# Half-length blocks for a chunked complex scan, with rotation tables read by broadcast

## The chip, the cores and the metric

The kernel runs on one core of one Trainium2 chip. The metric is the device time of the program in microseconds (us). Six runs of the kernel before took 205.23 to 207.02 us, with a median of 205.78 us.

The names used here: TensorE (PE in the profile) does matmuls and transposes and writes to PSUM. VectorE (DVE), ScalarE (ACT) and GpSimd (POOL) work on SBUF[...]. SyncE (SP) issues most of the DMAs. Each engine works through its own queue in order, and semaphores tie the queues together.

## The reference

The input x has 2048 rows of 512. It is normalised row by row, and three things are added: x itself, a diagonal complex state-space model (SSM) and a gated feed-forward network.

```python
def _A_ref(x, Lambda_re, Lambda_im, B_re, B_im, C_re, C_im, log_dt, Dskip):
    Lam = Lambda_re + 1j * Lambda_im
    dt = jnp.exp(log_dt)
    Lam_bar = jnp.exp(dt * Lam)
    B_bar = ((Lam_bar - 1.0) / Lam)[:, None] * (B_re + 1j * B_im)
    Bu = jnp.einsum("bld,pd->blp", x + 0j, B_bar)
    for t in range(L):                       # 2048 steps
        h = Lam_bar[None, :] * h + Bu[:, t, :]
    y = 2.0 * jnp.einsum("blp,dp->bld", hseq, C_re + 1j * C_im).real + x * Dskip

def _B_ref(x, w_gate, w_up, w_down):         # 512 -> 1376 -> 512
    return (_gelu(x @ w_gate) * (x @ w_up)) @ w_down

xn = _layernorm(x)
return x + _A_ref(xn, ...) + _B_ref(xn, ...)
```

The recurrence runs over the 2048 steps, separately for each of the 512 states.

## The kernel before

The 2048 steps are worked off in four chunks of CT = 512. States lie on partitions, 128 at a time, so there are KT = 4 groups of states, and time lies along the free dimension. One chunk of a state array is therefore a tile of 128 partitions by 4 x 512 = 2048 elements.

**The scan.** The complex recurrence is turned into two real ones. Each input is rotated back by the angle of its step, then a real scan with the factor r, the magnitude of Lam_bar, runs over the real and the imaginary part, and the result is rotated forward. Ct and St hold the cosine and sine of step times angle. Qc, Qs and nQs hold the forward rotation with the factor of B_bar folded in. coef holds r, with a zero at the first step of each state group, so that one scan instruction can run through all four groups. What is carried from one chunk to the next is the last column of the scan's results gre and gim, turned by the angle of a whole chunk and multiplied by r. It is added into the first column of the next chunk's input (lines 438 to 445).

**Setup.** Line 125 makes the row of step numbers (iota_f). The parameters arrive as a small tile vec_kp, which TensorE transposes (line 224) and VectorE copies to vec (226). From vec come dt (243, Exp), thn (245, turns per step), r (249, Exp), then turns, rounding and fraction (253 to 259), and Abs, Sin and Cos on ScalarE (276 to 281). B is transposed on TensorE in eight groups of four blocks (219) and copied out of PSUM (221), by VectorE or ScalarE, whichever the planner chose. Line 203 does the same for the normalised x of the first chunk; its PSUM pool holds one buffer, that of B's two.

**A chunk.** emit_v makes V, the input of the scan, in eight PSUM groups (real and imaginary part for each state group), which ScalarE copies out (363). emit_gu makes eleven pairs of groups, gate (372) and up (376), of four matmuls each. ScalarE takes the gelu of the gate (G, 381) and copies the up part (U, 382); VectorE multiplies them into H (388). All these groups share five PSUM buffers (ps_mm); G and U have three buffers each. The layer norm of chunks 2 and 3 is also done by ScalarE between them (173, 181), with its rstd by POOL (186). emit_ssm is VectorE's work: rotation (424 to 429), carry (438 to 445), two scans (448, 452), forward rotation into Hs (458 to 463). emit_output (399 to 406) adds everything up on TensorE, in four output groups of 24 matmul instructions a chunk, one chunk later: output of chunk c comes after V and gate/up of chunk c + 1.

**What sets the order.** The program is written engine-free of order; a planner puts each engine's instructions in a fixed sequence at build time, by its own estimates and by priorities. Blocks under hp() have a high priority and move ahead of ordinary ones as soon as the planner takes their inputs for ready. The order of a queue is then fixed, and an engine whose next instruction waits does nothing else.

Of the kernel before, what the change touches and what calls it, by code (L numbers as in the profile page):

```python
# [21 lines left out]
def kernel(  # L22
# [25 lines left out]
    CT = 512  # L48
    NCH = L // CT
    TPC = CT // P  # L50
    NFT = (F + P - 1) // P
    FSZ = [min(P, F - i * P) for i in range(NFT)]
    EPS = 1e-5
# [156 lines left out]
    ln_stats_dve(0)  # L210
    xnT_of[0] = ln_finish(0, use_pe=True)

    bT_re = const.tile([P, DC, NS], BF16, name="bT_re")
    bT_im = const.tile([P, DC, NS], BF16, name="bT_im")
    for bT, bn in ((bT_re, b_nat[0]), (bT_im, b_nat[1])):
        for dc in range(DC):
            pb = ps_b.tile([P, KT, P], BF16, name="pb", tag="b")
            for k in range(KT):
                nc.tensor.transpose(pb[:, k, :], bn[:, k, dc * P:(dc + 1) * P], ident[:])  # L219
            with hp():  # L220
                nc.any.tensor_copy(out=bT[:, dc, :], in_=pb[:].rearrange("p k q -> p (k q)"))

    pvec = ps_b.tile([P, 4 * KT], BF16, name="pvec", tag="b")
    nc.tensor.transpose(pvec[:], vec_kp[:], ident[0:4 * KT, 0:4 * KT])
    vec = small.tile([P, 4, KT], F32, name="vec")
    nc.vector.tensor_copy(out=vec[:].rearrange("p j k -> p (j k)"), in_=pvec[:])
    ps_b_cm.__exit__(None, None, None)
    lam_re = vec[:, 0, :]
    lam_im = vec[:, 1, :]
    logdt = vec[:, 2, :]  # L230
# [9 lines left out]
    nc.vector.memset(halfpi[:], math.pi / 2.0)  # L240

    dt = sm("dt")
    nc.scalar.activation(out=dt[:], in_=logdt, func=ACTF.Exp)
    thn = sm("thn")
    nc.vector.scalar_tensor_tensor(out=thn[:], in0=dt[:], scalar=INV_2PI, in1=lam_im, op0=ALU.mult, op1=ALU.mult)  # L245
    a_re = sm("a_re")
    nc.vector.tensor_tensor(out=a_re[:], in0=dt[:], in1=lam_re, op=ALU.mult)
    r = sm("r")
    nc.scalar.activation(out=r[:], in_=a_re[:], func=ACTF.Exp)

    turns = setup.tile([P, KT, CT], F32, name="turns")
    for k in range(KT):
        nc.vector.tensor_scalar(out=turns[:, k, :], in0=iota_f[:], scalar1=thn[:, k:k + 1], scalar2=None,
                                op0=ALU.mult)
    kk = setup.tile([P, KT, CT], F32, name="kk")
    nc.vector.tensor_scalar(out=kk[:], in0=turns[:], scalar1=ROUND_MAGIC, scalar2=ROUND_MAGIC,
                            op0=ALU.add, op1=ALU.subtract)
    frac = kk
    nc.vector.tensor_tensor(out=frac[:], in0=turns[:], in1=kk[:], op=ALU.subtract)
    th2 = sm2("th2")  # L260
    nc.vector.tensor_copy(out=th2[:, 0:KT], in_=thn[:])
    nc.vector.tensor_scalar(out=th2[:, KT:2 * KT], in0=thn[:], scalar1=float(CT), scalar2=None, op0=ALU.mult)
    k2 = sm2("k2")
    nc.vector.tensor_scalar(out=k2[:], in0=th2[:], scalar1=ROUND_MAGIC, scalar2=ROUND_MAGIC,
                            op0=ALU.add, op1=ALU.subtract)
    fr2 = sm2("fr2")
    nc.vector.tensor_tensor(out=fr2[:], in0=th2[:], in1=k2[:], op=ALU.subtract)

    afrac = turns
    St = const.tile([P, KT, CT], BF16, name="St")  # L270
    Ct = const.tile([P, KT, CT], BF16, name="Ct")
    afr2 = sm2("afr2")
    sn2 = sm2("sn2")
    cs2 = sm2("cs2")
# [8 lines left out]
    s1 = sn2[:, 0:KT]  # L283
    cTt = cs2[:, KT:2 * KT]
    sTt = sn2[:, KT:2 * KT]

    for c in range(1, min(N_DVE_LN, NCH)):
        ln_stats_dve(c)
# [35 lines left out]
    nf2im = sm("nf2im")  # L324
    nc.vector.tensor_scalar(out=nf2im[:], in0=f2im[:], scalar1=-1.0, scalar2=None, op0=ALU.mult)

    Qc = const.tile([P, KT, CT], BF16, name="Qc")
    Qs = const.tile([P, KT, CT], BF16, name="Qs")
    nQs = const.tile([P, KT, CT], BF16, name="nQs")
    coef = const.tile([P, KT, CT], F32, name="coef")  # L330
    qt = setup.tile([P, KT, CT], F32, name="qt")
    qt2 = setup.tile([P, KT, CT], F32, name="qt2")

    def emit_tables():
        for k in range(KT):
            nc.vector.tensor_scalar(out=qt[:, k, :], in0=St[:, k, :], scalar1=nf2im[:, k:k + 1], scalar2=None,
                                    op0=ALU.mult)
            nc.vector.tensor_scalar(out=qt2[:, k, :], in0=Ct[:, k, :], scalar1=f2im[:, k:k + 1], scalar2=None,
                                    op0=ALU.mult)
        for k in range(KT):  # L340
            nc.vector.scalar_tensor_tensor(out=Qc[:, k, :], in0=Ct[:, k, :], scalar=f2re[:, k:k + 1],  # L341
                                           in1=qt[:, k, :], op0=ALU.mult, op1=ALU.add)
            nc.vector.scalar_tensor_tensor(out=Qs[:, k, :], in0=St[:, k, :], scalar=f2re[:, k:k + 1],  # L343
                                           in1=qt2[:, k, :], op0=ALU.mult, op1=ALU.add)
        nc.vector.tensor_scalar(out=nQs[:], in0=Qs[:], scalar1=-1.0, scalar2=None, op0=ALU.mult)
        for k in range(KT):
            nc.vector.tensor_scalar(out=coef[:, k, :], in0=iota_f[:], scalar1=0.0, scalar2=r[:, k:k + 1],
                                    op0=ALU.mult, op1=ALU.add)
        nc.vector.memset(coef[:, :, 0:1], 0.0)

# [61 lines left out]

    g_prev = [None]

    def emit_ssm(c, V):
        vre = V[:, :, 0, :]
        vim = V[:, :, 1, :]
        m1 = rot.tile([P, KT, CT], BF16, name="m1")
        m2 = rot.tile([P, KT, CT], BF16, name="m2")
        m3 = rot.tile([P, KT, CT], BF16, name="m3")  # L420
        m4 = rot.tile([P, KT, CT], BF16, name="m4")
        ure = m1
        uim = m3
        nc.vector.tensor_tensor(out=m1[:], in0=Ct[:], in1=vre, op=ALU.mult)  # L424
        nc.vector.tensor_tensor(out=m2[:], in0=St[:], in1=vim, op=ALU.mult)
        nc.vector.tensor_tensor(out=ure[:], in0=m1[:], in1=m2[:], op=ALU.add)
        nc.vector.tensor_tensor(out=m3[:], in0=Ct[:], in1=vim, op=ALU.mult)
        nc.vector.tensor_tensor(out=m4[:], in0=St[:], in1=vre, op=ALU.mult)
        nc.vector.tensor_tensor(out=uim[:], in0=m3[:], in1=m4[:], op=ALU.subtract)
        if g_prev[0] is not None:  # L430
            gre_p, gim_p = g_prev[0]
            glr = gre_p[:, :, CT - 1]
            gli = gim_p[:, :, CT - 1]
            ca = stat.tile([P, KT], F32, name="ca")
            cb = stat.tile([P, KT], F32, name="cb")
            rire = stat.tile([P, KT], F32, name="rire")
            riim = stat.tile([P, KT], F32, name="riim")
            nc.vector.tensor_tensor(out=ca[:], in0=rcT[:], in1=glr, op=ALU.mult)
            nc.vector.tensor_tensor(out=cb[:], in0=rsT[:], in1=gli, op=ALU.mult)
            nc.vector.tensor_tensor(out=rire[:], in0=ca[:], in1=cb[:], op=ALU.subtract)  # L440
            nc.vector.tensor_tensor(out=ca[:], in0=rsT[:], in1=glr, op=ALU.mult)
            nc.vector.tensor_tensor(out=cb[:], in0=rcT[:], in1=gli, op=ALU.mult)
            nc.vector.tensor_tensor(out=riim[:], in0=ca[:], in1=cb[:], op=ALU.add)
            nc.vector.tensor_tensor(out=ure[:, :, 0], in0=ure[:, :, 0], in1=rire[:], op=ALU.add)
            nc.vector.tensor_tensor(out=uim[:, :, 0], in0=uim[:, :, 0], in1=riim[:], op=ALU.add)
        gre = gpool.tile([P, KT, CT], BF16, name="gre")
        gim = gpool.tile([P, KT, CT], BF16, name="gim")
        nc.vector.tensor_tensor_scan(out=gre[:].rearrange("p k t -> p (k t)"),  # L448
                                     data0=coef[:].rearrange("p k t -> p (k t)"),
                                     data1=ure[:].rearrange("p k t -> p (k t)"),  # L450
                                     initial=0.0, op0=ALU.mult, op1=ALU.add)
        nc.vector.tensor_tensor_scan(out=gim[:].rearrange("p k t -> p (k t)"),  # L452
                                     data0=coef[:].rearrange("p k t -> p (k t)"),
                                     data1=uim[:].rearrange("p k t -> p (k t)"),
                                     initial=0.0, op0=ALU.mult, op1=ALU.add)
        g_prev[0] = (gre, gim)
        Hs = hspool.tile([P, KT, 2, CT], BF16, name="Hs")
        nc.vector.tensor_tensor(out=m1[:], in0=Qc[:], in1=gre[:], op=ALU.mult)
        nc.vector.tensor_tensor(out=m2[:], in0=Qs[:], in1=gim[:], op=ALU.mult)
        nc.vector.tensor_tensor(out=Hs[:, :, 0, :], in0=m1[:], in1=m2[:], op=ALU.subtract)  # L460
        nc.vector.tensor_tensor(out=m3[:], in0=nQs[:], in1=gre[:], op=ALU.mult)
        nc.vector.tensor_tensor(out=m4[:], in0=Qc[:], in1=gim[:], op=ALU.mult)
        nc.vector.tensor_tensor(out=Hs[:, :, 1, :], in0=m3[:], in1=m4[:], op=ALU.subtract)
        return Hs

    pending = None
# [54 lines left out]
```

## Time and profile before

| | us |
|---|---|
| median of six runs | 205.78 |
| the profiled execution | 205.88 |
| its span, first to last instruction | 204.1 |
| TensorE busy | 184.5 (90%) |
| VectorE busy | 141.3 (69%) |
| ScalarE busy | 99.8 (49%) |
| POOL busy | 4.5 (2%) |
| first V matmul | 14.43 |
| V of the second chunk begins | 47.09 |
| first output group begins | 75.67 |
| mean granted TensorE clock | 0.983 |

The profile is one execution. Its strip of 40 slices shows the busy share of each engine in tenths, with the granted clock of TensorE in a row of its own. A row of groups names line, engine, operation, output<-inputs, shapes and count; behind the first bar stand total busy us and the mean ns of one, behind the second the idle time of the engine just before, with what ended it. The mean of one instruction is a little longer than the step from its start to the next one's: a VectorE product of 2048 elements has 1.22 us, and the next one starts 1.14 us after it. The table of waits adds up that idle time by who waited for whom. The chain of waits goes back from the last instruction to whatever released it, step by step.

### The profile page before, as it was taken

To read this page: it belongs to the slowest core of one execution; us is meant where nothing else is said; L and a number is where in the kernel's file an instruction comes from. 1 tells how busy PE (TensorE), PEld (TensorE's weight loads), DVE (VectorE), ACT (ScalarE), POOL (GpSimd) and SP (SyncE) were. 2 spreads that over 40 slices of the span, in tenths; PEclk is the share of its full clock that TensorE was granted. 3 is DMA by queue.
4 is the path that set the end of the run, shared out by engine and by line. 5 is a ranking of instruction groups with operands and counts; after the bars stand their busy time and mean duration, and the time that the engine had idled before them with its cause. 6 is when DMAs were issued, how large, how long until landed. Compare 5 with 4: busy or idle time off the path is not lost.

```text
span 204.1 us, 2468 instructions
## 1 busy us (share of the span) xinstructions
PE 184.5 (90%) x897; PEld 88.4 (43%) x915; DVE 141.3 (69%) x235; ACT 99.8 (49%) x187; POOL 4.5 (2%) x8
## 2 busy tenths in 40 slices
PE   1489749999997899999999999999999999999992
PEld 0364313444443344444444454444444444444441
DVE  6699899989999999991198999600699995000000
ACT  2176999897652644114998424116665541111111
POOL 0100100020000000000002000000000000000000
PEclk9999957999999999999999999999999999999999
DMA  5999972000002200103000040000000000001000
GB/s 168 315 386 358 212 165 51 2 0 0 3 0 43 60 0 0 50 31 112 16 0 5 8 97 26 26 29 26 0 0 0 3 0 26 26 26 54 26 26 27
DMA packets 19772, 12.25 MB, mean 60 GB/s; under 512 B 11216, under 2 KB 19760, under 8 KB 19760
## 3 DMA queue, kind: packets, MB, share of 16 engines
q1 hardware_dynamic: 19728, 12.10, 21.7%
q8 instruction: 7, 0.11, 0.2%
q14 instruction: 5, 0.04, 0.1%
q10 hardware_dynamic: 32, 0.00, 0.0%
HBM read 7.38 MB, written 2.10 MB: 46 GB/s over the span
## 4 chain that ended last, share of the span: by engine, by line
PE 64%; DVE 27%; DMA 2%; issue 2%; ACT 1%; POOL 1%; SPq 1%; ACTq 0%; DVEq 0%; POOLq 0%
PE po L399 19%; PE pu L376 10%; PE pg L372 10%; PE po L403 7%; PE pv L360 7%; PE po L402 6%; DVE H L388 2%; DMA bre_nat<-in_A_B_re_dram 2%; DVE gim L452 2%; DVE gre L448 2%; PE po L406 2%; PE po L404 2%; DVE Qs L343 1%; DVE Qc L341 1%; DVE xn L194 1%
## 5 line engine op out<-in xcount | busy, mean ns | idle before, releaser
L376 PE MATMUL pu<-xnT,wu 128*128 128x512 bf16 (+1 forms) x174 | 46.5, 389 | 6.7 <-ACT V L363 4.2
L372 PE MATMUL pg<-xnT,wg 128*128 128x512 bf16 (+1 forms) x172 | 45.3, 383 | 0.2
L399 PE MATMUL po<-wd,H 128*128 128x512 bf16 (+1 forms) x174 | 40.5, 379 | 0.1
L381 ACT ACTIVATE G<-pg 128x512 bf16<-128x512 f32 (+1 forms) x44 | 26.6, 605 | 27.1 <-DVE H L388 19.3
L410 ACT CAST osb<-po 128x512 bf16<-128x512 f32 x16 | 9.4, 587 | 52.7 <-PE po L406 52.7
L376 PEld LDWEIGHTS <-wu 128*128 128x128 bf16 (+1 forms) x176 | 17.9, 102 | 28.4 <-issue 9.2
L382 ACT CAST U<-pu 128x512 bf16<-128x512 f32 (+1 forms) x44 | 25.9, 590 | 4.3 <-PE pu L376 4.0
L372 PEld LDWEIGHTS <-wg 128*128 128x128 bf16 (+1 forms) x176 | 17.8, 101 | 21.4 <-issue 1.6
L403 PE MATMUL po<-cT_im,Hs 128*128 128x512 bf16 x64 | 24.2, 378 | 0.3
L399 PEld LDWEIGHTS <-H 128*128 128x128 bf16 (+1 forms) x176 | 16.7, 98 | 17.6
L363 ACT CAST V<-pv 128x512 bf16<-128x512 f32 x32 | 18.5, 584 | 7.3 <-PE pv L360 7.3
L402 PE MATMUL po<-cT_re,Hs 128*128 128x512 bf16 x58 | 22.0, 379 | 0.0
L388 DVE TENSOR_TENSOR H<-G,U 128x512 bf16<-128x512 bf16 (+1 forms) x44 | 18.0, 413 | 0.0
L360 PE MATMUL pv<-xnT,bT_re 128*128 128x512 bf16 x62 | 16.3, 379 | 0.8 <-DVE thn L245 0.7
L360 PE MATMUL pv<-xnT,bT_im 128*128 128x512 bf16 x62 | 16.2, 379 | 0.1
L424 DVE TENSOR_TENSOR m_1722<-Ct,V 128x2048 bf16<-128x2048 bf16 x1 | 1.2, 1226 | 13.9 <-ACT V L363 13.9
L403 PEld LDWEIGHTS <-Hs 128*128 128x128 bf16 x64 | 6.2, 97 | 7.6
L360 PEld LDWEIGHTS <-bT_im 128*128 128x128 bf16 x64 | 6.3, 98 | 7.5
L402 PEld LDWEIGHTS <-Hs 128*128 128x128 bf16 x64 | 6.2, 98 | 7.6
L360 PEld LDWEIGHTS <-bT_re 128*128 128x128 bf16 x64 | 6.2, 98 | 7.6 <-issue 0.7
L424 DVE TENSOR_TENSOR m_1362<-Ct,V 128x2048 bf16<-128x2048 bf16 x1 | 1.2, 1224 | 8.8 <-ACT V L363 8.8
L219 PE MATMUL pb<-ident,bre_nat 128*128 128x128 bf16 x16 | 2.2, 307 | 4.8 <-DMA bre_nat<-in_A_B_re_dram 4.3
(158 smaller groups left out, 198.9 us busy)
## 6 DMA issues: line engine op xcount, KB each, us to landing
out_dram<-osb SPq DMA_DIRECT2D x16, 128.0 KB, 1.7
x_c<-in_A_x_dram SPq DMA_DIRECT2D x3, 512.0 KB, 6.0
wd<-in_B_w_down_dram SPq DMA_DIRECT2D x1, 1280.0 KB, 12.9
wg<-in_B_w_gate_dram SPq DMA_DIRECT2D x1, 736.0 KB, 10.9
wu<-in_B_w_up_dram SPq DMA_DIRECT2D x1, 736.0 KB
wg<-in_B_w_gate_dram SPq DMA_DIRECT2D x1, 640.0 KB, 8.4
wu<-in_B_w_up_dram SPq DMA_DIRECT2D x1, 640.0 KB
x_c<-in_A_x_dram SPq DMA_DIRECT2D x4, 128.0 KB, 2.4
```

Of the source, the lines that this page charges most:

```text
L360: nc.tensor.matmul(pv[:], lhsT=bT[:, dc, k * P:(k + 1) * P], rhs=xnT[:, dc, :], start=(dc == 0), stop=(dc == DC - 1))
L363: nc.scalar.copy(out=V[:, k, part, :], in_=pv[:])
L372: nc.tensor.matmul(pg[0:fs, :], lhsT=wg[:, dc, ft * P:ft * P + fs], rhs=xnT[:, dc, :], start=(dc == 0), stop=(dc == DC - 1))
L376: nc.tensor.matmul(pu[0:fs, :], lhsT=wu[:, dc, ft * P:ft * P + fs], rhs=xnT[:, dc, :], start=(dc == 0), stop=(dc == DC - 1))
L381: nc.scalar.activation(out=G[0:fs, :], in_=pg[0:fs, :], func=ACTF.Gelu_apprx_tanh)
L382: nc.scalar.copy(out=U[0:fs, :], in_=pu[0:fs, :])
L388: nc.vector.tensor_tensor(out=H[0:fs, ft, :], in0=G[0:fs, :], in1=U[0:fs, :], op=ALU.mult)
L399: nc.tensor.matmul(po[:], lhsT=H[0:fs, ft, tsl], rhs=wd[0:fs, ft, :], start=first, stop=False)
L402: nc.tensor.matmul(po[:], lhsT=Hs[:, k, 0, tsl], rhs=cT_re[:, k, :], start=False, stop=False)
L403: nc.tensor.matmul(po[:], lhsT=Hs[:, k, 1, tsl], rhs=cT_im[:, k, :], start=False, stop=False)
L404: nc.tensor.matmul(po[:], lhsT=ident[:], rhs=x_tiles[c][:, i, :], start=False, stop=False)
L410: nc.scalar.copy(out=osb[:], in_=po[:])
```

## The change

The chunk stays at 512 steps, but the scan inside it goes by blocks of TB = 256 steps, NH = 2 to a chunk.

- All tables (Ct, St, Qc, Qs, nQs, coef and what they are made of) have 256 steps instead of 512. The whole-block angle is that of 256 steps.
- The eight table multiplies per chunk read a table twice, through a view (bc) with a step of zero over the two halves. V and Hs keep their layout and are read and written through a matching view (hk). The tiles m1 to m4, gre and gim are laid out half by half.
- Each scan is done in two instructions of 1024 elements, with a carry before each but the very first.
- In the text of the setup, the eight groups of B's transposes stand behind the parameter work and the tables; the parameter copy, dt, thn and the angle work stand under hp().

The first lines below set the new sizes; the parameter and angle part follows, then the tables, then the scan. Left out are the lines where only CT turned into TB in a shape and the unchanged formulas.

```diff
+    TB = 256
+    NH = CT // TB
...
-    bT_re = const.tile([P, DC, NS], BF16, name="bT_re")
-    bT_im = const.tile([P, DC, NS], BF16, name="bT_im")
-    for bT, bn in ((bT_re, b_nat[0]), (bT_im, b_nat[1])):
...
     pvec = ps_b.tile([P, 4 * KT], BF16, name="pvec", tag="b")
     nc.tensor.transpose(pvec[:], vec_kp[:], ident[0:4 * KT, 0:4 * KT])
     vec = small.tile([P, 4, KT], F32, name="vec")
-    nc.vector.tensor_copy(out=vec[:].rearrange("p j k -> p (j k)"), in_=pvec[:])
-    ps_b_cm.__exit__(None, None, None)
+    with hp():
+        nc.vector.tensor_copy(out=vec[:].rearrange("p j k -> p (j k)"), in_=pvec[:])
...
-    nc.scalar.activation(out=dt[:], in_=logdt, func=ACTF.Exp)
+    with hp():
+        nc.scalar.activation(out=dt[:], in_=logdt, func=ACTF.Exp)
+        nc.vector.scalar_tensor_tensor(out=thn[:], in0=dt[:], scalar=INV_2PI, in1=lam_im, op0=ALU.mult,
+                                       op1=ALU.mult)
...
-    turns = setup.tile([P, KT, CT], F32, name="turns")
-    for k in range(KT):
-        nc.vector.tensor_scalar(out=turns[:, k, :], in0=iota_f[:], scalar1=thn[:, k:k + 1], ...
+    with hp():
+        turns = setup.tile([P, KT, TB], F32, name="turns")
+        for k in range(KT):
+            nc.vector.tensor_scalar(out=turns[:, k, :], in0=iota_f[:, 0:TB], scalar1=thn[:, k:k + 1], ...
+        kk = setup.tile([P, KT, TB], F32, name="kk")
...
+        nc.vector.tensor_scalar(out=th2[:, KT:2 * KT], in0=thn[:], scalar1=float(TB), scalar2=None, op0=ALU.mult)
...
+    bT_re = const.tile([P, DC, NS], BF16, name="bT_re")
+    bT_im = const.tile([P, DC, NS], BF16, name="bT_im")
+    for bT, bn in ((bT_re, b_nat[0]), (bT_im, b_nat[1])):
+        for dc in range(DC):
+            pb = ps_b.tile([P, KT, P], BF16, name="pb", tag="b")
+            for k in range(KT):
+                nc.tensor.transpose(pb[:, k, :], bn[:, k, dc * P:(dc + 1) * P], ident[:])
+            with hp():
+                nc.any.tensor_copy(out=bT[:, dc, :], in_=pb[:].rearrange("p k q -> p (k q)"))
+    ps_b_cm.__exit__(None, None, None)
...
+    def bc(tab):
+        return tab[:].unsqueeze(1).to_broadcast([P, NH, KT, TB])
+
+    def hk(ap3):
+        return ap3.rearrange("p k (h t) -> p h k t", h=NH)
+
     def emit_ssm(c, V):
-        vre = V[:, :, 0, :]
-        m1 = rot.tile([P, KT, CT], BF16, name="m1")
+        vre = hk(V[:, :, 0, :])
+        m1 = rot.tile([P, NH, KT, TB], BF16, name="m1")
...
-        nc.vector.tensor_tensor(out=m1[:], in0=Ct[:], in1=vre, op=ALU.mult)
+        nc.vector.tensor_tensor(out=m1[:], in0=bc(Ct), in1=vre, op=ALU.mult)
...
+        for h in range(NH):
+            if g_prev[0] is not None:
+                glr, gli = g_prev[0]
...
+                nc.vector.tensor_tensor(out=ure[:, h, :, 0], in0=ure[:, h, :, 0], in1=rire[:], op=ALU.add)
+                nc.vector.tensor_tensor(out=uim[:, h, :, 0], in0=uim[:, h, :, 0], in1=riim[:], op=ALU.add)
+            nc.vector.tensor_tensor_scan(out=gre[:, h].rearrange("p k t -> p (k t)"),
+                                         data0=coef[:].rearrange("p k t -> p (k t)"),
+                                         data1=ure[:, h].rearrange("p k t -> p (k t)"),
+                                         initial=0.0, op0=ALU.mult, op1=ALU.add)
...
+            g_prev[0] = (gre[:, h, :, TB - 1], gim[:, h, :, TB - 1])
...
-        nc.vector.tensor_tensor(out=Hs[:, :, 0, :], in0=m1[:], in1=m2[:], op=ALU.subtract)
+        nc.vector.tensor_tensor(out=hk(Hs[:, :, 0, :]), in0=m1[:], in1=m2[:], op=ALU.subtract)
```

## The prediction

> **What bounds the kernel now.** First the page's slices, 5.1 us each: who is full, and when.
>
> ```profile
> PE   1489749999997899999999999999999999999992
> DVE  6699899989999999991198999600699995000000
> ACT  2176999897652644114998424116665541111111
> PEclk9999957999999999999999999999999999999999
> ```
>
> TensorE is full from about 75 us to the end. VectorE (DVE) is full up to about 92 us, then has gaps. TensorE's holes are at 24 to 36 us, where its clock dips, and at 62 to 73 us. Then the table of waits: engine, line, what it waited for, total us, times, longest.
>
> ```profile
> ACT G L381 <- DVE H L388: 19.3, 12, 4.4
> DVE m_1722 L424 <- ACT V L363: 13.9, 1, 13.9
> DVE m_1362 L424 <- ACT V L363: 8.8, 1, 8.8
> PE pu L376 <- ACT V L363: 4.2, 1, 4.2
> PE pu L376 <- ACT G L381: 2.4, 4, 1.4
> ```
>
> Rows four and five are all that TensorE loses after its start, with the half clock that follows the 4.2. In that 4.2 ScalarE did the Sin tables while PSUM stood full. The 2.4 has a longer tail: gelu G needs a buffer that product H on VectorE frees (first row). Rows two and three are VectorE's slack in the last two chunks. The chain of waits says the same in order of time (start, us, what):
>
> ```profile
> 47.58 4.33 DVE gre L448
> 51.91 0.32 DVE H L388
> 52.23 4.33 DVE gim L452
> ...
> 72.00 0.35 DVE H L388
> ...
> 72.43 0.61 ACT G L381
> ...
> 73.08 1.02 PE pu L376 x4
> ```
>
> VectorE's queue sets the time to 73 us, and TensorE alone sets it from there. So the change is worth what it takes from VectorE ahead of the product H that frees TensorE, and work saved after 75 us is worth nothing.
>
> **The change, part by part.** Rows for the prices (mean ns after the "|"):
>
> ```profile
> L448 DVE TENSOR_TENSOR_SCAN gre<-coef,m_598 128x2048 bf16<-128x2048 f32 x1 | 4.4, 4414 | 0.0
> L125 DVE TENSOR_TENSOR_SCAN iota_f<-ones_f 128x512 f32<-128x512 f32 x1 | 1.2, 1224 | 0.0
> L424 DVE TENSOR_TENSOR m_598<-Ct,V 128x2048 bf16<-128x2048 bf16 x1 | 1.2, 1218 | 0.0
> L259 DVE TENSOR_TENSOR kk<-turns,kk 128x2048 f32<-128x2048 f32 x1 | 2.3, 2272 | 0.0
> L341 DVE SCALAR_TENSOR_TENSOR Qc<-Ct,f2re,qt 128x512 bf16<-128x512 bf16 x4 | 3.0, 742 | 0.0
> L280 ACT ACTIVATE St<-kk 128x2048 bf16<-128x2048 f32 x1 | 1.9, 1894 | 0.0
> ```
>
> (1) Tables half as long. VectorE's start-to-start steps lose half of their per-element part: four turns 0.40 to 0.27 (0.5 saved), rounding 1.14 to 0.61 (0.5), the L259 subtract 2.19 to 1.12 (1.1), four coef (0.5), eight qt/qt2 (1.1), eight Qc/Qs 0.665 to 0.40 (2.1), nQs (0.3): 6.1 us, all ahead of 38 us on the bounding queue. ScalarE: Abs, St and Ct lose 0.85 each, 2.6 us.
>
> (2) Scans in halves. From 512 and 2048 elements a scan costs 2.08 ns an element and 0.16 us fixed, so 1024 take 2.29, 2.20 start to start. Four for two of 4.33: +0.14 per chunk. The carry of eight 4-column operations ran from 73.73 to 74.55 plus one more, 0.90 us. There is one more per chunk: +0.90. Together +1.04 per chunk, 2.1 in the two chunks that bound; in the others it falls into gaps of 8.8 and 13.9.
>
> (3) Broadcast multiplies, eight per chunk, 32 in all. No row of before reads a table twice with a zero step. [...] A gain is excluded, since element count and types stay. L424 already reads V in separate runs of 512 at that speed, so I take 1.22. [...]
>
> (4) Setup reordered. B's 32 transposes move behind the parameters in the text, so TensorE does them before those of xn. In the new order VectorE does turns, rounding, subtraction (2.9 us) before the first xn; all four xnT copies are on VectorE, each waiting for a transpose that waits for the previous copy (one PSUM buffer). Walked: xn starts at 12.4 (9.2 before), last xnT copy at 17.0, first V matmul at 17.4 (14.4 before). TensorE starts 3.0 late.
>
> (5) Sin ahead of V. The angle is ready at 12.3, so ScalarE does Abs, table load, St and Ct from 13.1 to 17.6, before V needs it. Exp for r then comes after Sin: one more table load, 1.28, to 18.9. V's evictions start there, at most two groups behind, inside five PSUM buffers. So the 4.2 wait goes and the half-clock groups after it go. TensorE runs eight V groups and 22 gate/up groups (0.863 each) from 17.4 to 43.35; before it was at this point, the next chunk's V, at 47.09. That is 3.7 us, which counts only if VectorE follows.
>
> (6) VectorE's walk, in its new order. After the last xnT copy come the second chunk's statistics, a 1.4 us wait for POOL's rstd, xn, small operations: qt starts at 23.9 (27.3 before). Tables take 5.4 us instead of 9.1: 29.4, where before stood at 37.8 with four H already done. The first H is at 30.5 (32.4). From there chunk 0 has 13.6 us of products, 8.8 of scans, 0.9 carry, 11 H of 0.33, 1.3 xn: chunk 1's first multiply starts at 57.7 (65.2 before), 7.5 us ahead.
>
> (7) Which H frees TensorE. An up group n waits for G of n-2 (five PSUM buffers), and G for H three earlier, so the last up group of chunk 1 waits for the sixth H. Before, this H stood ahead of both scans, at 73.4. In the new order it stands behind two half scans and most of a carry: 57.7 + six multiplies and adds 6.8 + five H 1.7 + first carry 0.9 + two half scans 4.4 + 0.3 = 71.8. So 1.6 remains of the 7.5. G follows 0.5 later, the up group 0.65 after that, at 73.0; the first output group at 73.84, where the trace of before has 75.67. On the way TensorE stalls 1.2 at 47 (eighth H of chunk 0), 1.3 at 62, 0.8 at 70 and 1.2 at 73. After that it is full again; chunk 2 stalls for 0.2, as this walk gives for before too (where it puts the first output at 75.77).
>
> Sum: 75.77 - 73.84 = 1.9 us of span; 204.1 - 1.9 = 202.2. The profiled execution took 205.88, 1.78 around its span: 204.0, and since it lay 0.10 above the median of 205.78, **203.9**.
>
> What speaks against it is the clock. The row: after 2.3 us without matmuls the granted clock fell, and stayed at half to 33 us (start:end, length, busy by engine, then PEclk).
>
> ```profile
> 26.00:27.00 1.00, 0.00 (x0) 0.00 (x0) 0.83 (x7) 1.00 (x1) 0.00 (x0) 0.67 0.87 188
> 28.00:33.00 5.00, 4.48 (x11) 1.62 (x12) 5.00 (x12) 4.97 (x10) 0.00 (x0) 0.50 0.60 125
> ```
>
> Yet before's first V matmuls ran at full clock straight from the transposes. [...]
>
> **The rivals.** [...]
>
> [...]
>
> *More passes through* (199.3 to 202.6). If the H products were not kept behind the half scans, TensorE's four stalls of 4.6 us would go: 203.9 - 4.6 = 199.3. Against: the order in the queue is fixed by the build.
>
> **How the numbers follow.** I give 0.66 to the gain of 1.9 (202.6 to 204.75), 0.06 to more, 0.12 to the gain given back within bounds of no change, 0.06 to given back beyond that by start and clock together, and 0.10 to the lost mode. About 0.5% (1.03 us) is what a measurement of this kernel can tell from no change: below 204.75 counts as faster, above 206.8 as slower. So faster 0.72, same 0.12, slower 0.16. The range leaves out the lost mode and most of "more": 202.4 to 206.8.
>
> **What the profile after would show.** L424's counterpart at about 1220 ns (right) or 2270 (lost mode); half scans at 2290; four table loads on ScalarE; the wait of the up group for V gone; first V matmul near 17.4 and full clock there; next chunk's V at 43 to 44; the first output group at 73.8. [...] If the first output group comes at 73.8 and the end doesn't move with it, a wait in chunk 2 or 3, from H's place behind the carry, has eaten the gain, and the prediction is wrong in step 7.

## The result, and the profile after

The changed kernel takes 204.09 us (median of ten runs, 203.63 to 205.28); the kernel before took 205.96 us (twenty runs) beside it. The ratio is 0.991, with a 95% interval of 0.989 to 0.994. The forecast was 203.9 us and faster. The span of the profiled execution fell from 204.1 to 202.4 us.

The first output group starts at 74.00 us instead of 75.67. From there to the end of the span it takes 128.4 us in both kernels, so the whole gain is made before that point. The strip of 40 slices, now 5.06 us each:

```profile
PE   1658999999997879999999999999999999999992
DVE  6997999998999999900298999700799996000000
ACT  2497599957626434114998441116676432111111
PEclk9999999999999999999999999999999999999999
```

TensorE's hole of before at 24 to 36 us is gone. Its hole from about 61 us on is no smaller. The table of waits says the same:

```profile
ACT G L389 <- DVE H L396: 14.8, 11, 4.1
DVE m_1390 L438 <- ACT V L371: 13.4, 1, 13.4
DVE m_1764 L438 <- ACT V L371: 12.8, 1, 12.8
...
PE pu L384 <- ACT G L389: 2.8, 3, 1.1
```

No up group waits for V any more (4.2 us before). What TensorE still waits for is a gelu G whose buffer an H has not yet freed: 2.8 us, where it was 2.4 before. The costliest rows give the prices of the new pieces:

```profile
L461 DVE TENSOR_TENSOR_SCAN gre<-coef,m_598 128x1024 bf16<-128x1024 f32 x2 | 4.6, 2282 | 0.0
L349 DVE SCALAR_TENSOR_TENSOR Qc<-Ct,f2re,qt 128x256 bf16<-128x256 bf16 x4 | 1.9, 479 | 0.0
L438 DVE TENSOR_TENSOR m_598<-Ct,V 128x2048 bf16<-128x2048 bf16 x1 | 1.2, 1218 | 0.0
L254 DVE TENSOR_TENSOR kk<-turns,kk 128x1024 f32<-128x1024 f32 x1 | 1.2, 1217 | 0.0
```

A multiply that reads its table twice costs 1.22 us, exactly what it cost when the table had full length (1218 ns for m_598 in both kernels). That settles the point that could have cost most: the forecast gave 0.10 to multiplies of 2270 ns. The chain of waits (start, us, what) up to the first output group:

```profile
43.20 2.92 POOL rstd L188
...
66.86 2.21 DVE gre L461
69.14 0.32 DVE H L396
69.47 2.20 DVE gim L465
72.06 0.35 DVE H L396
72.49 0.61 ACT G L389
73.14 1.02 PE pu L384 x4
```

As foreseen, the sixth H of the second chunk now stands behind two half scans, and TensorE's last up group waits for it. Before, it stood ahead of both scans, and there it was not the one that bound:

```profile
71.92 0.42 DVE L388 TENSOR_TENSOR H<-G,U 128x512 bf16<-128x512 bf16 x1
73.08 1.02 PE L376 MATMUL pu<-xnT,wu 128*128 128x512 bf16 x4 [0.21 <-ACT G L381]
73.39 0.42 DVE L388 TENSOR_TENSOR H<-G,U 128x512 bf16<-128x512 bf16 x1
74.81 1.03 PE L376 MATMUL pu<-xnT,wu 128*96 128x512 bf16 x4
```

In the kernel before, the fifth H (71.92) released the up group that waited last (73.08). The sixth (73.39) let the last up group start at about 74.55, and TensorE came to it only at 74.81.

One thing was not foreseen: GpSimd's rstd is on the chain, with 2.92 us where it took 1.04 before. Yet VectorE's own wait for it is no longer than before: 0.83 us, and it was 0.90 us at 45.95 in the kernel before.

### The profile page after: what moved, and what is told of

It reads as the page before. It is cut to its first block, busy times and chain, and to the rows that moved or that the text cites. A ratio compares the mean times of both kernels' runs of the same rounds, so it can differ in the third digit from the quotient of the medians.

```text
span 202.4 us, 2507 instructions
## 1 busy us (share of the span) xinstructions
PE 185.8 (92%) x897; PEld 88.7 (44%) x915; DVE 138.6 (68%) x276; ACT 98.0 (48%) x187; POOL 6.5 (3%) x8
## 4 chain that ended last, share of the span: by engine, by line
PE 67%; DVE 26%; ACT 3%; POOL 1%; issue 1%; ACTq 0%
PE po L407 19%; PE pv L368 11%; PE pu L384 10%; PE pg L380 9%; PE po L411 7%; PE po L410 6%; DVE gim L465 3%; DVE H L396 3%; DVE gre L461 2%; DVE bst L161 2%; PE po L414 2%; PE po L412 2%; POOL rstd L188 1%; DVE xn L196 1%; ACT G L389 1%
## 5 line engine op out<-in xcount | busy, mean ns | idle before, releaser
L384 PE MATMUL pu<-xnT,wu 128*128 128x512 bf16 (+1 forms) x174 | 44.9, 379 | 3.0 <-ACT G L389 2.8
L380 PE MATMUL pg<-xnT,wg 128*128 128x512 bf16 (+1 forms) x172 | 44.6, 379 | 0.2
L389 ACT ACTIVATE G<-pg 128x512 bf16<-128x512 f32 (+1 forms) x44 | 26.8, 610 | 29.3 <-DVE H L396 14.8
L368 PE MATMUL pv<-xnT,bT_re 128*128 128x512 bf16 x62 | 17.9, 407 | 0.8 <-DVE xnT L205 0.5
L368 PE MATMUL pv<-xnT,bT_im 128*128 128x512 bf16 x62 | 17.0, 395 | 0.1
L188 POOL TENSOR_TENSOR rstd<-ve,mhalf 128x4 f32<-128x4 f32 x2 | 4.1, 2054 | 86.7 <-DVE m_1392 L460 62.0
```

Of the source, the lines that this page charges most:

```text
L188: nc.gpsimd.tensor_tensor(out=st["rstd"][:], in0=st["ve"][:], in1=mhalf[:], op=ALU.pow)
L368: nc.tensor.matmul(pv[:], lhsT=bT[:, dc, k * P:(k + 1) * P], rhs=xnT[:, dc, :], start=(dc == 0), stop=(dc == DC - 1))
L380: nc.tensor.matmul(pg[0:fs, :], lhsT=wg[:, dc, ft * P:ft * P + fs], rhs=xnT[:, dc, :], start=(dc == 0), stop=(dc == DC - 1))
L384: nc.tensor.matmul(pu[0:fs, :], lhsT=wu[:, dc, ft * P:ft * P + fs], rhs=xnT[:, dc, :], start=(dc == 0), stop=(dc == DC - 1))
L389: nc.scalar.activation(out=G[0:fs, :], in_=pg[0:fs, :], func=ACTF.Gelu_apprx_tanh)
```

## The experiments

Eight kernels were run in two groups of four. The kernel before had a median of 205.59 us (23 runs) beside the first group and 205.86 us (11 runs) beside the second. "Sixth H" is the sixth H of the second chunk; with three buffers its last up group can't start without it.

### The reordered setup alone

The changed kernel with the block length set back to the chunk, so that tables and scans have 512 steps and only the order of the setup differs from before.

```diff
-    TB = 256
+    TB = CT
```

> The changed kernel with its setup in the new order, but with tables, scans and multiplies of 512 steps as before (TB = 512, so one block to a chunk and no repeated table). Theory (Sin ahead of V takes the 4.2 us wait away, and where a product H stands in VectorE's queue decides the rest): the reorder alone gives as much as the whole change or a little more, since the scans stay whole and fewer carries stand ahead of H: 203.0 to 203.9, first output group near 73. Rival (the shorter tables bring the gain, and the reorder only makes TensorE start late): 205.5 to 207.

Measured: 205.97 us, ratio 1.002 (1.000 to 1.004). The theory missed, and the rival was right. Part of TensorE's timeline (start, us, operation, the idle time before it in brackets):

```profile
18.73 0.61 PE L368 MATMUL pv<-xnT,bT_re 128*128 128x512 bf16 x1 [0.52 <-DVE xnT L205]
...
22.11 1.91 PE L368 MATMUL pv<-xnT,bT_re 128*128 128x512 bf16 x4
...
66.33 1.02 PE L384 MATMUL pu<-xnT,wu 128*128 128x512 bf16 x4 [2.54 <-ACT G L389]
```

V starts 4.3 us later than before, and its first groups run at half rate (1.7 us from start to start instead of 0.86). The wait at V is gone. The two cancel: the next chunk's V begins at 47.23, and before at 47.09. Taking the wait away by starting later is worth nothing here.

### The blocks alone

The changed kernel with the text of the setup in the order of before: B's transposes first, no high priority for parameters and angles.

```diff
+    bT_re = const.tile([P, DC, NS], BF16, name="bT_re")
...
     pvec = ps_b.tile([P, 4 * KT], BF16, name="pvec", tag="b")
-    with hp():
-        nc.vector.tensor_copy(out=vec[:].rearrange("p j k -> p (j k)"), in_=pvec[:])
+    nc.vector.tensor_copy(out=vec[:].rearrange("p j k -> p (j k)"), in_=pvec[:])
...
-    with hp():
+    if True:
         turns = setup.tile([P, KT, TB], F32, name="turns")
```

> Tables, scans and multiplies of 256 steps as in the changed kernel, but the setup in the order of before. Theory: Sin still stands in the middle of V's evictions, but takes 2.6 us less, so the 4.2 us wait shrinks to about 1.9 and may stay short of the half clock; the time is 203.0 to 204.0. So the two parts do not add up: each alone gives what both give. Rival (they add up, and share the gain of 1.9): this one and the reorder alone lose together 1.9 against before, so that this one is 204.5 to 205.5.

Measured: 202.12 us, ratio 0.983 (0.980 to 0.987). The direction of the theory holds, and the size is larger than it said: the blocks alone gain 3.5 us, and with the reorder only 1.9 are left.

```profile
13.81 1.02 PE L365 MATMUL pv<-xnT,bT_re 128*128 128x512 bf16 x3 [0.67 <-ACT xnT L205]
14.67 1.03 PE L365 MATMUL pv<-xnT,bT_im 128*128 128x512 bf16 x4
...
22.73 1.02 PE L377 MATMUL pg<-xnT,wg 128*128 128x512 bf16 x4 [1.86 <-ACT V L368]
```

V starts at 13.81, at full rate from the first group (0.86 us from start to start). The wait at V is still there, but with 256-step tables the three passes of ScalarE ahead of V's last evictions (Abs, St, Ct) take 3.2 us instead of 5.8, so it is 1.86 us and not 4.2, and the groups right after it run at full rate (22.73 to 23.59). The next chunk's V begins at 41.72, 3.1 us ahead of the changed kernel.

VectorE reaches the second chunk no earlier (first multiply at 58.23, against 57.93), so why does it end earlier? In the order that the build fixed here, the sixth H stands behind one half scan only (why the planner put it there, no run shows):

```profile
67.54 2.29 DVE L458 TENSOR_TENSOR_SCAN gre<-coef,m 128x1024 bf16<-128x1024 f32 x1
69.75 0.40 DVE L393 TENSOR_TENSOR H<-G,U 128x512 bf16<-128x512 bf16 x1
70.27 2.29 DVE L462 TENSOR_TENSOR_SCAN gim<-coef,m 128x1024 bf16<-128x1024 f32 x1
```

It starts at 69.75, against 71.98.

### Fewer operations on VectorE

The second carry of each chunk is left out: the state at the end of a chunk's first half is not handed to its second half.

```diff
-            if g_prev[0] is not None:
+            if g_prev[0] is not None and h == 0:
```

> The changed kernel without the carry into the second half of each chunk: eight small operations per chunk fewer on VectorE, 3.6 us in all (what is left out is the state passed from one half block to the next). Rival (the sum of VectorE's work ahead of 73 us decides): 1.8 us less in the two chunks that bound, so 202.3. Theory (the place of the product H in the queue decides): without the carry the planner sets the two halves' scans closer together and H of chunk 1 farther behind, four TensorE stalls grow, and with less work the kernel is slower than the changed one: 205.5 to 206.7.

Measured: 205.12 us, ratio 0.999 (0.996 to 1.001). VectorE has 32 operations less, and the kernel is 1 us slower than the changed one. The order is drawn up anew with any change, and here both gre scans and one gim scan came ahead of the sixth H, which starts at 73.54, 1.56 later than in the changed kernel. Of these 1.56, VectorE was 0.42 late already when it began the second chunk (58.35 against 57.93); the rest is the order. The theory's direction is right, the lower end of its range was 0.4 too high, and the rival fell. What counts here is where this one H stands, not how much work there is.

### Six buffers each for G and U

```diff
-    gup = ctx.enter_context(tc.tile_pool(name="gup", bufs=3))
+    gup = ctx.enter_context(tc.tile_pool(name="gup", bufs=6))
```

> The changed kernel with six buffers for G and for U instead of three; nothing else. Theory (G waits for the H three earlier, and this alone stalls TensorE at 61, 69 and 72 us): the three stalls of 1.14, 0.65 and 1.04 go, and those of chunk 2 and 3, if any; TensorE runs without a stall from its first V group on, and the time is 199.0 to 201.3, below both kernels. Rival (VectorE's sum of work bounds up to 73 us, whatever the buffers): 203.5 to 204.5, with the wait moved from G to PSUM or to Hs.

Measured: 200.31 us, ratio 0.973 (0.970 to 0.977), inside the theory's range. In its profile no gate or up group waits at all, and the first output group starts at 69.33. G still has 14.8 us of waits for H in the changed kernel; here 0.6 are left, and what G waits for is TensorE:

```profile
ACT G L389 <- PE pg L380: 6.1, 25, 0.3
...
ACT G L389 <- DVE H L396: 0.6, 1, 0.6
```

VectorE's queue kept its order: the sixth H starts at 71.51, about as in the changed kernel, but now 2.2 us after the first output group. So ahead of the output, VectorE's lateness reaches TensorE through these three buffers and in no other way. G and U got their buffers together; the run doesn't tell them apart.

### The blocks with six buffers

The second experiment's kernel with the buffers of the fourth.

> The 256-step blocks with the setup order of before, and six buffers each for G and U. Theory (the reordered setup costs time whether or not the buffers bind): with six buffers TensorE's only stall is the one at V, about 1.9 us near 23 us, so an early start counts one for one. V starts near 13.8 at full clock, first output group at 67.5 to 68.5, median 198.5 to 199.8, that is 0.5 to 1.8 below the kernel with the reorder and six buffers. Rival (the reorder pays once the buffers no longer bind, since it takes the wait at V away): 200.3 or more, first output group at 69.3 or later.

Measured: 197.79 us (197.74 to 197.90), ratio 0.961 (0.959 to 0.964). It is the fastest kernel of the study, 6.3 us below the changed one, and a bit below the range of the theory. The first output group starts at 67.68. Its start:

```profile
19.92 1.03 PE L365 MATMUL pv<-xnT,bT_im 128*128 128x512 bf16 x4
22.79 1.02 PE L377 MATMUL pg<-xnT,wg 128*128 128x512 bf16 x4 [1.85 <-ACT V L368]
```

The first gate group starts at 22.79 here and at 24.43 in the kernel with the reorder and six buffers. That difference of 1.64 is the difference of the first output groups (1.65) and of the spans (1.7). The medians differ by 2.5, because the profiled execution of the kernel with the reorder (199.58) was faster than its median (200.31). That the reorder pays once buffers no longer bind is refuted.

### TensorE kept busy before V

The kernel with the reorder and six buffers, and 16 matmuls whose results nobody uses, spread among the transposes of xn.

```diff
+    pw = ps_b.tile([P, KT * P], F32, name="pw", tag="b")
...
+        nc.tensor.matmul(pw[:], lhsT=ident[:], rhs=bT_im[:, wi % DC, :], start=True, stop=True)
```

> The changed kernel with six buffers each for G and U, and 16 extra matmuls of 128x512 (results not used) among the transposes of xn before V. Theory (V starts at half rate because TensorE was idle between sparse transposes): V's groups take 0.86 from the first one; the median falls by 0.5 to 1.7 against the same kernel without the extra matmuls (200.3), to 198.6 to 199.8. Rival (the clock is tied to something else, or the extra matmuls only delay the transposes): V's first groups still take 1.7 each or V starts over 1 us later, 200.3 or more.

Measured: 200.45 us, ratio 0.973 (0.971 to 0.976): no gain. Yet V does what the theory said:

```profile
15.80 0.81 PE L295 MATMUL pw<-bT_im,ident 128*128 128x512 bf16 x3
16.48 0.38 PE L203 MATMUL pt<-ident,xn 128*128 128x128 bf16 x4
...
17.48 1.04 PE L371 MATMUL pv<-xnT,bT_re 128*128 128x512 bf16 x4 [0.39 <-DVE xnT L205]
18.35 1.03 PE L371 MATMUL pv<-xnT,bT_im 128*128 128x512 bf16 x4
```

V runs at full rate from its first group (0.87 us from start to start), and four transposes take 0.38 us instead of 0.59. But V starts at 17.48 instead of 16.45, and the first gate group falls on the same moment (24.39, against 24.43). That V now starts later is not the reason for its full rate: with the reorder alone V started later still, at 18.73, and ran slow. From 12.00 to 16.30 TensorE was busy for 4.25 us here, and for 2.17 us with the reorder and six buffers alone. Theory and rival were each half right: behind a TensorE that was kept busy V was not slow, and the cure costs as much as it brings.

### Four buffers in the kernel before

```diff
-    gup = ctx.enter_context(tc.tile_pool(name="gup", bufs=3))
+    gup = ctx.enter_context(tc.tile_pool(name="gup", bufs=4))
```

> The kernel before with four buffers each for G and U instead of three (six don't fit beside the tables of 512 steps). Theory (H late on VectorE stalls TensorE through the buffers of G in the kernel before too): one more buffer moves the waits one H earlier, 1.5 to 2.2 us faster, 203.4 to 204.1. Rival (in the kernel before only the wait at V matters): no change, 205.2 to 206.

Measured: 203.43 us, ratio 0.990 (0.987 to 0.992), inside the theory's range. The wait at V is untouched, and the waits for G shrink from 2.4 to 1.3:

```profile
PE pu L376 <- ACT V L363: 4.1, 1, 4.1
PE pu L376 <- ACT G L381: 1.3, 3, 0.6
```

This profile doesn't show the buffer's effect alone. The first output group is 2.5 us earlier (73.19 against 75.67), and 1.6 of that stand at the second chunk's V already (45.52 against 47.09): the wait at V ended 0.7 earlier, and the slow matmuls after it lasted less long. The runs help here. In three of the six the mean granted clock was 0.981 to 0.983, as in most runs of the kernel before; they took 203.44, 204.24 and 204.32 us, and the eight such runs of before had a median of 205.90. So some 1.6 us or more don't come from a shorter slow stretch. One more buffer on the kernel before does about as much as the whole change.

### The small product on GpSimd

The changed kernel with the product of mean and rstd for chunks 2 and 3 on GpSimd, so that VectorE does not wait for rstd.

```diff
-            nc.vector.tensor_tensor(out=st["nmr"][:], in0=st["nmean"][:], in1=st["rstd"][:], op=ALU.mult)
+            nc.gpsimd.tensor_tensor(out=st["nmr"][:], in0=st["nmean"][:], in1=st["rstd"][:], op=ALU.mult)
```

> The changed kernel with the small product of mean and rstd for chunks 2 and 3 computed by GpSimd instead of VectorE, so that VectorE doesn't wait for GpSimd's rstd when that runs long beside a half scan. Theory (the 0.83 us that VectorE waited at 45 us is on the path that sets the end): the wait goes, first output group up to 0.8 earlier, median 203.2 to 203.9. Rival (it is absorbed by the stalls behind it): 204.1, within 0.3.

Measured: 203.02 us, ratio 0.988 (0.984 to 0.991). The median is 1.07 below the changed kernel's and 0.2 below the theory's range; the intervals of the two ratios touch, so the traces carry the reading. VectorE's timeline of the changed kernel, and then of this one:

```profile
43.03 2.28 DVE L461 TENSOR_TENSOR_SCAN gre<-coef,m_598 128x1024 bf16<-128x1024 f32 x1
46.15 0.16 DVE L189 TENSOR_TENSOR nmr<-nmean,rstd 128x4 f32<-128x4 f32 x1 [0.83 <-POOL rstd L188]
46.23 0.42 DVE L396 TENSOR_TENSOR H<-G,U 128x512 bf16<-128x512 bf16 x1
```

```profile
42.83 2.28 DVE L461 TENSOR_TENSOR_SCAN gre<-coef,m 128x1024 bf16<-128x1024 f32 x1
45.03 0.40 DVE L396 TENSOR_TENSOR H<-G,U 128x512 bf16<-128x512 bf16 x1
```

The H that follows is 1.2 us earlier: 0.2 were there already, the rest is the wait and the small product. Nothing absorbs it: the sixth H starts at 70.89 instead of 71.98, and the first output group at 72.91 instead of 74.00.

### One relation through all of them

| kernel | H that the last up group needs | wait of that group | first output group | difference |
|---|---|---|---|---|
| changed | 71.98 | 1.04 | 74.00 | 2.02 |
| product on GpSimd | 70.89 | 1.05 | 72.91 | 2.02 |
| second carry left out | 73.54 | 0.63 | 75.55 | 2.01 |
| before, four buffers (the fifth H) | 71.17 | 0.21 | 73.19 | 2.02 |
| blocks alone | 69.75 | 0.05 | 71.75 | 2.00 |
| reorder alone | 73.83 | 0.02 | 75.84 | 2.01 |

In the first four, the end of the kernel hangs on one product of 0.4 us and its place in VectorE's queue. The last two rows don't test this, because there the last up group hardly waits. Earlier stalls (2.24 at 60.52 with slow matmuls behind it, and 2.54 at 66.33) brought TensorE to the same point at nearly the same moment; these waits, too, are for a G whose buffer an H frees, the first H of the chunk. With six buffers none of this binds, and the start of TensorE decides.

## Why the prediction was right, and where it was not

**Steps 1 to 3, the prices**, hold. Half scans took 2.28 to 2.29 (2.29 said), table operations came out at the stated half prices (start to start: turns 0.26, rounding 0.60, the subtract 1.14, Qc and Qs 0.40), and the broadcast multiplies at 1.20 to 1.23 (1.22 said, from the row of L424). A carry took 0.8 and not 0.90.

**Step 4.** V was to start at 17.4 and started at 16.38. The first xn stood at 11.3 and not at 12.4; B's load had landed about 1.1 us earlier than in the profile of before, and the queues moved with it. The landing was taken as fixed from one execution.

**Step 5, wrong in the clock.** The text took from the trace of before that V would run at full rate. There V's groups start 0.86 us apart from the first one on:

```profile
14.43 1.02 PE L360 MATMUL pv<-xnT,bT_re 128*128 128x512 bf16 x3 [0.67 <-DVE thn L245]
15.29 1.03 PE L360 MATMUL pv<-xnT,bT_im 128*128 128x512 bf16 x4
16.15 1.03 PE L360 MATMUL pv<-xnT,bT_re 128*128 128x512 bf16 x4
```

In the changed kernel V starts at half rate, 1.7 us from group to group:

```profile
16.38 0.61 PE L368 MATMUL pv<-xnT,bT_re 128*128 128x512 bf16 x1 [0.52 <-DVE xnT L205]
17.20 1.06 PE L368 MATMUL pv<-xnT,bT_re 128*128 128x512 bf16 x2 [0.22 <-issue]
18.06 1.91 PE L368 MATMUL pv<-xnT,bT_im 128*128 128x512 bf16 x4
19.77 1.88 PE L368 MATMUL pv<-xnT,bT_re 128*128 128x512 bf16 x4
21.47 1.03 PE L368 MATMUL pv<-xnT,bT_im 128*128 128x512 bf16 x4
```

The eight groups need 25.80 - 16.38 = 9.4 us, where 8 x 0.863 = 6.9 would do: 2.5 lost. The next chunk's V stood at 44.79; 43.35 was said, which is 1.0 gained by the earlier start and 2.5 lost. The granted clock gave no warning either: its record shows 1.00 in this stretch although the matmuls run at half rate (changed kernel first, then the blocks alone; start:end, length, busy by engine PE, PEld, DVE, ACT and POOL with counts, then PEclk):

```profile
16.40:21.40 5.00, 4.78 (x11) 1.76 (x13) 3.91 (x24) 2.99 (x5) 1.01 (x1) 1.00 1.10 340
```

```profile
16.40:21.40 5.00, 4.47 (x21) 1.95 (x20) 4.26 (x22) 4.60 (x8) 1.01 (x1) 1.00 1.11 336
```

Eleven matmuls against 21 in the same 5 us, under the same recorded clock. In the kernel before, TensorE was busy for 3.62 of the 4.40 us ahead of V (10.03 to 14.43), in the changed kernel for 2.12 of 4.40 (11.98 to 16.38); this difference should have weighed more. At the end the loss cost little: TensorE came late to where it would have stalled, and the stall of 1.2 at 47 us is missing in the trace. It was not quite free. The chain of waits of the changed kernel runs through the slow V, then the gelu, and reaches VectorE at an H that waited 0.45 us for its U:

```profile
17.20 8.77 PE pv L368 x30
...
30.07 0.42 DVE H L396
```

The length of the slow stretch differs from profile to profile: V's groups lost between 1.1 and 2.7 us (below), which at half rate is a stretch of about 2.2 to 5.4 us (an estimate: twice the loss).

**Step 5, wrong in the credit.** It counted the removal of the wait at V as 3.7 us for the reorder. The runs show that the halved tables alone cut this wait to 1.86 without a slow stretch after it, and that the reorder pays for the rest with a V that starts 2.6 us later and runs slow. It is worth nothing alone and costs 1.6 to 2.0 us beside the blocks (by the ratios 0.983 and 0.991, or by the medians). The sum for the whole change came out right; its division between the two parts was wrong.

**Step 6.** VectorE was early at first (qt at 22.34 for 23.9 said, first H at 29.20 for 30.5) and level by the second chunk (57.93 for 57.7). In between it lost 0.45 waiting for a U and 0.83 for rstd, plus 0.08 for the product behind it. Neither wait is in the walk, although the trace of before has one for rstd at the same place (0.90). That the error of step 4 and these two cancelled was luck. (The walk's 57.7 comes out if its terms are added to 29.4, the end of the tables, and not to the first H.)

**Step 7** held in place and size: the sixth H at 71.98 for 71.8, the first output group at 74.00 for 73.84, stalls of 1.14 at 62.49, 0.65 at 70.21 and 1.04 at 73.14 for 1.3, 0.8 and 1.2. Nothing in chunks 2 and 3 ate the gain. Its comparison with before was off: it held the sixth H at 73.4 to be the one that bound there, and that was the fifth. The forecast doesn't rest on it, since it sets one walk against the other (75.77, and the trace has 75.67).

**The rivals.** What the forecast calls the lost mode, with a chance of 0.10, is a broadcast multiply of 2270 ns, the price of the f32 subtract of 2048 elements (2272 ns); no run shows one, and all 32 took 1.20 to 1.23 us. To a gain given back it gave 0.12 and 0.06, on an estimate of the clock that no run shows; V did run at half rate and lost 2.5 us, and the gain stayed. "More passes through" (199.3) was argued from stalls that could not go while the order stood (they add up to 4.5 us, not 4.6). They could: with six buffers they went, and the time was 200.31.

What stays open is the scatter of the slow start. V's eight groups lost 2.5 us in this profile, 2.6 with the reorder alone, 2.7 with the second carry left out, 1.8 with the product on GpSimd and 1.1 with six buffers; no run here shows what sets the moment of the change.

## What to carry to other kernels

When a faster engine frees buffers for another, find the one instruction that releases the consumer, and its place in the queue: work saved elsewhere on the engine may be worth nothing, and another buffer may be worth more than the saving. Tables that shrink also free memory, and here three more buffers in that memory brought 3.8 us on top of the change, which itself brought 1.9 (3.5 without the reorder). A wait that is removed by starting later has to be weighed against the start, and a TensorE that had been busy for only half of the 4.4 us ahead of V lost 1.1 to 2.7 us here, which the trace of a dense start did not show.

## What the runs showed of the hardware

**GpSimd beside VectorE.** The same 4-column rstd on GpSimd took between 1.01 and 2.92 us, by what VectorE was doing when it started:

```profile
43.20 2.92 POOL L188 TENSOR_TENSOR rstd<-ve,mhalf 128x4 f32<-128x4 f32 x1 [24.70 <-DVE riim L458]
```

```profile
43.26 1.01 POOL L188 TENSOR_TENSOR rstd<-ve,mhalf 128x4 f32<-128x4 f32 x1 [24.36 <-DVE cb L451]
```

The first is the changed kernel, the second the blocks with six buffers.

| VectorE at the start of rstd | it ends | rstd starts | rstd takes | rstd ends after it |
|---|---|---|---|---|
| half scan (changed) | 45.31 | 43.20 | 2.92 | 0.81 |
| multiply of 2048 (reorder alone) | 45.15 | 44.17 | 1.84 | 0.86 |
| product H (before) | 109.88 | 109.55 | 1.19 | 0.86 |
| nothing (blocks alone) | | 43.20 | 1.01 | |

In each case it ended 0.8 to 0.9 us after VectorE's instruction, as if it had begun only then. What holds it up, no run shows. So a scan or multiply put ahead of VectorE's own wait did not hide that wait: VectorE waited 0.83 us behind the half scan, 0.90 behind the multiply and behind H, and 1.05 where it had been doing nothing. The run with the product on GpSimd shows what such a wait can cost.

**The record of the granted clock** shows 1.00 over a stretch at the start in which matmuls take twice their time (16.40 to 21.40 in the changed kernel, 1.7 us a group), while after TensorE's long wait in the kernel before it fell with them (0.50 from 28 to 33 us). The distance from one group's start to the next (0.86 or 1.7 here) is the surer sign.
